# A hand-ordered first stretch with two weight tiles in conversion, 32-column query products, and u stored from the scalar queue

## The chip, the cores and the metric

The kernel runs on one core of a Trainium2 chip. The metric is the device time of one execution in microseconds (us): the median of the runs shown, lower is better. A difference of about 0.5% is what a measurement of this kernel can tell from no change.

## What is computed

Three blocks follow one another, in float32: attention through 32 landmarks, then two mixers with a two-layer perceptron (MLP) each. The weights `U`, `V`, `w_ch1`, `w_ch2` arrive as float64 and are converted on the chip.

```python
# attention: q, k, v are (8, 8, 576, 64); q_lm, k_lm are means over 18 rows (32 landmarks)
A  = softmax(q    @ k_lm^T / 8)          # 576 x 32
Bm = softmax(q_lm @ k_lm^T / 8)          # 32 x 32
C  = softmax(q_lm @ k^T    / 8)          # 32 x 576
Z  = Bm^T / (norm1(Bm) * norminf(Bm))
for _ in range(6): Z = 2 * Z - Z @ Bm @ Z
x  = A @ Z @ C @ v                       # heads side by side: (8, 576, 512)
# mixer 1: a rank-32 product over the sequence, then the MLP
u  = x + (x^T @ U @ V)^T
x  = u + relu(u @ w_ch1) @ w_ch2         # 512 -> 2048 -> 512
# mixer 2: real part of a 2-d FFT, layer norm, then a second MLP
u  = x + real(fft2(x));  un = layernorm(u)
out = u + relu(un @ w2_ch1) @ w2_ch2
```

## The kernel before, in words

**The work.** The attention runs batch by batch (class `Batch`, eight batches). The MLPs run over nine chunks of 512 columns (`NC`, `NCH`), the 8 x 576 rows of the sequence laid end to end. Each MLP takes two passes, since half of its weights fit at a time: passes 0 and 1 are the first MLP, passes 2 and 3 the second. A chunk has eight up blocks (`Mlp.up`, L205, 12 matmuls of 128x512 each, L212 to L214) and four down blocks (L248 to L272, 24 matmuls each, L257 to L259). Each matrix is held as a high part and a rest, so each product is three matmuls. `Mlp.stream` (L221) is a generator: one step for each up block and two for each down block, `STEPS` = 16 for a chunk.

**The conversion.** A weight tile of 128x512 is converted by `convert` (L87): a DMA into the raw tile `wraw`, four DVE operations (L97, L98, L101, L104), one ACT operation (L102), an addition on POOL (L106), a DVE operation (L108), then a cast on ACT and a subtraction on POOL in `split` (L51, L52). Its scratch tiles `cva` and `cvp` have one buffer each. In pass 0, `direct` (L880) converts 16 tiles straight into the MLP's weights. The tiles of the later passes are converted by `stage` (L113) and put in DRAM.

**The order.** Batch 0 and the first half of batch 1 run in 32 steps before the MLP starts (`FIRST`, L888, the loop at L896). There the Tile scheduler orders the instructions of each engine by its own costs. From L903 on, `tc.manual_schedule()` keeps the order of the program. In each step the loop runs one step of the MLP, the attention steps that `Slots` has for it (`Batch.steps`, L619: pairs of a step number and a method), and some conversion steps. Batch b starts 16 (b - 2) steps after the MLP does, so that batch b + 1 runs beside chunk b.

**The hand-over from a batch to a chunk.** `Batch.mix` (L601) makes four tiles `u1T` of 128x576; ACT (L609) and DVE (L610) each copy one half out of PSUM. Then SP issues the store to `u1`: three stores of 128 rows (L612, L614), one of 127 rows (L616) and one of one row (L617), because the rows of `u` have an order of their own. The chunk's tiles `xf` come back from `u1` by SP (L139, `ByBatch.get`), and `split_x` (L193) makes the high part on ACT (L51) and the rest on DVE or POOL (L52). Two of the four splits of the next chunk stand in the down block d = 2, and two in d = 3.

**The query products.** `query` (L486) multiplies blocks of 128 query columns by the landmarks (L498), and `mixed` (L543) multiplies the attention weights by `U` (L550), both with 128 columns of weights at a time. `values` (L467) makes its products with 32 columns of weights (L479), each into another 32 partitions of the result.

Of the kernel before, what the change touches and what calls it, by code (L numbers as in the profile page):

```python
# [23 lines left out]
P = 128  # L24
# [15 lines left out]
def body(ctx: ExitStack, tc: tile.TileContext, qT, kT, vn, mU, mV, w11, w12, w21, w22,  # L40
# [13 lines left out]
    def from_f64(pool, dst, w, n, pp=P):  # L54
# [3 lines left out]
        a = pool.tile([P, 512], U32, name="cva", bufs=1)[0:pp, 0:n]  # L58
        p = pool.tile([P, 512], U32, name="cvp", bufs=1)[0:pp, 0:n]
# [27 lines left out]
    def convert(cv, src, out, lag=0):  # L87

        raw = cv.tile([P, 512], U64, name="wraw", bufs=2)
        nc.sync.dma_start(raw, src)  # L90
        yield 1
        yield from wait(lag)
        u = raw.bitcast(U32).rearrange("p (n two) -> p n two", two=2)
        lo, hi = u[:, :, 0], u[:, :, 1]
        a = cv.tile([P, 512], U32, name="cva", bufs=1)
        p = cv.tile([P, 512], U32, name="cvp", bufs=1)
# [8 lines left out]
        yield 1  # L105
# [7 lines left out]
    def stage(cv, src, dst):  # L113
        st = cv.tile([P, 2, 512], F32R, name="stg", bufs=1)
        yield from convert(cv, src, st, 4)
        yield from wait(1)
        nc.sync.dma_start(dst, f32(st))
# [45 lines left out]
    class Mlp:  # L163
# [36 lines left out]
        def start(self):  # L200
            self.nx = []
            self.xf = self.load(0, self.passes[0][0])
            yield from self.split_x(self.xf)
# [85 lines left out]
    def attention_constants(cp, t):  # L289
        nc.sync.dma_start(ident_sb, ident)  # L290
        for nm, src, n in (("mask", mask, 64), ("bones", bones, P), ("istack", istack, R)):
            t[nm] = cp.tile([P, n], F32, name=nm + "_sb")
            nc.sync.dma_start(t[nm], src)
        t["U"] = cp.tile([P, 5, R], F32, name="U_sb")
# [3 lines left out]
        for nm in ("kb", "qb"):  # L298
            t[nm] = cp.tile([P, 4, 64], F32, name=nm)
            nc.gpsimd.memset(t[nm], 0.0)  # L300
# [5 lines left out]
    def attention_setup(t, pool, cvp):  # L306
        uraw = cvp.tile([P, 512], U64, name="wraw", bufs=2)[:, 0:5 * R].rearrange("p (t r) -> p t r", r=R)
# [5 lines left out]
        vst = pool.tile([P, S], F32, name="E", bufs=2)[0:R]  # L313
        for n in range(3):
            c = slice(n * S // 3, (n + 1) * S // 3)
            vraw = cvp.tile([P, 512], U64, name="wraw", bufs=2)[0:R, 0:S // 3]
# [8 lines left out]
    class Batch:  # L325
# [5 lines left out]
        EJ = [slice(0, 64), slice(64, P)]  # L331

# [127 lines left out]
        def scores_tail(self):  # L460
# [4 lines left out]
            nc.vector.tensor_copy(self.ETt, ps[0:64, 0:2 * P].rearrange("p (g c) -> p g c", g=2))  # L465
# [20 lines left out]
        def query(self, n):  # L486
# [528 lines left out]
```

## Time and profile before

| | |
|---|---|
| median of 3 runs | 2053.39 us (2045.59 to 2053.95) |
| the profiled execution | 2051.87 us |
| its span | 2050.1 us |
| busy, share of the span | PE 94%, DVE 46%, ACT 26%, POOL 17% |
| granted TensorE clock, mean | 0.979 of full speed |
| DMA | 262 MB, mean 128 GB/s |

The span is the time from the first to the last instruction that the profiler saw; about 1.8 us lie around it. PE, PEld, DVE, ACT, POOL and SP are the engines: matmul, weight load, vector, scalar, GpSimd and the queue that issues most DMAs. An L number is a line of the kernel. PE is busy nearly all the time from 220 us on. Before that, the page's slices of 51 us show it at four to eight tenths.

### The profile page before, as it was taken

What the parts mean: (1) busy time and instruction counts of PE and PEld (TensorE: products, weight loads), DVE (VectorE), ACT (ScalarE), POOL (GpSimd) and SP (SyncE); (2) the same over time, 40 slices, a digit from 0 to 9 for tenths busy, and PEclk for the clock granted to TensorE, in tenths of its full rate; (3) what the DMA queues carried; (4) which work ended last, traced back from release to release, by engine and by line L of the source; (5) the groups of instructions that cost most, each with busy time, mean ns of one, the idle gap of its engine ahead of it and who ended that gap; (6) DMA issues with size and microseconds to landing.
All of it is one profiled execution on the core that took longest, in us unless ns stands there. A gap on an engine that the chain in (4) does not pass through costs nothing.

```text
span 2050.1 us, 24963 instructions
## 1 busy us (share of the span) xinstructions
PE 1936.9 (94%) x9656; PEld 1578.3 (77%) x9656; DVE 949.0 (46%) x1682; ACT 532.8 (26%) x1089; POOL 358.4 (17%) x346
## 2 busy tenths in 40 slices
PE   4848999999999989999999999999999999999998
PEld 3636777877877878888788787888788888888887
DVE  5664744655553333454654654654432223333333
ACT  2332322322221222232332323433322221111110
POOL 2241110111111112222322222222111110000000
PEclk9869999999999999999999999999999999999999
DMA  5332352244212563343543663432422452432322
GB/s 179 118 129 76 101 163 93 101 137 145 91 57 94 175 233 126 131 150 101 178 149 106 236 226 99 157 125 79 151 82 83 170 185 93 125 122 88 93 93 77
DMA packets 145863, 262.17 MB, mean 128 GB/s; under 512 B 22768, under 2 KB 77904, under 8 KB 145744
## 3 DMA queue, kind: packets, MB, share of 16 engines
q1 hardware_dynamic: 145744, 260.58, 37.7%
q8 instruction: 76, 1.25, 0.3%
q14 instruction: 43, 0.35, 0.1%
HBM read 166.93 MB, written 93.59 MB: 127 GB/s over the span
## 4 chain that ended last, share of the span: by engine, by line
PE 74%; DVE 5%; DMA 5%; issue 4%; SPq 2%; POOL 1%; ACT 1%; DVEq 0%; POOLq 0%; ACTq 0%
PE ps L212 11%; PE ps L214 11%; PE ps L213 11%; PE ps L257 10%; PE ps L259 10%; PE ps L258 10%; DMA xf<-u 4%; SPq L617 1%; PE ps_f L77 1%; PE ps_f L76 1%; PE ps_f L78 1%; PE ps_n L607 1%; PE ps_n L566 1%; POOL x L52 1%; PE ps_c L440 1%
## 5 line engine op out<-in xcount | busy, mean ns | idle before, releaser
L212 PE MATMUL ps<-x,w 128*128 128x512 f32 x1152 | 465.9, 404 | 11.5 <-DVE g L217 6.6
L257 PE MATMUL ps<-g,w 128*128 128x512 f32 x1152 | 462.6, 402 | 2.0 <-DVE g L217 2.0
L214 PE MATMUL ps<-x,w 128*128 128x512 f32 x1152 | 454.5, 395 | 3.8 <-POOL x L52 1.8
L213 PE MATMUL ps<-x,w 128*128 128x512 f32 x1152 | 452.3, 393 | 0.0
L259 PE MATMUL ps<-g,w 128*128 128x512 f32 x1152 | 451.8, 392 | 0.0
L258 PE MATMUL ps<-g,w 128*128 128x512 f32 x1152 | 451.2, 392 | 0.0
L217 DVE SCALAR_TENSOR_TENSOR g<-ps,g 128x512 fp32r<-128x512 f32 x288 | 198.7, 690 | 461.6 <-ACT g L216 461.4
L216 ACT ACTIVATE g<-ps 128x512 fp32r<-128x512 f32 x288 | 171.8, 597 | 699.1 <-PE ps L214 698.7
L212 PEld LDWEIGHTS ps<-x,w 128*128 128x128 f32 x1152 | 218.8, 190 | 61.2 <-DVE g L217 7.0
L214 PEld LDWEIGHTS ps<-x,w 128*128 128x128 f32 x1152 | 218.0, 189 | 57.1 <-POOL x L52 6.6
L257 PEld LDWEIGHTS ps<-g,w 128*128 128x128 f32 x1152 | 217.7, 189 | 50.6 <-issue 4.4
L259 PEld LDWEIGHTS ps<-g,w 128*128 128x128 f32 x1152 | 217.6, 189 | 47.5
L213 PEld LDWEIGHTS ps<-x,w 128*128 128x128 f32 x1152 | 219.0, 190 | 43.2
L258 PEld LDWEIGHTS ps<-g,w 128*128 128x128 f32 x1152 | 218.1, 189 | 43.2
L52 POOL TENSOR_TENSOR x<-xf,x 128x512 fp32r<-128x512 f32 x72 | 97.0, 1352 | 633.7 <-ACT x L51 625.2
L266 DVE TENSOR_TENSOR xf<-ps,xf 128x512 f32<-128x512 f32 x108 | 74.4, 689 | 239.7 <-PE ps L259 236.9
L106 POOL TENSOR_TENSOR cvp<-cvp,cva 128x512 f32<-128x512 f32 x64 | 84.7, 1323 | 470.8 <-DVE cvp L104 456.9
L52 DVE TENSOR_TENSOR x<-xf,x 128x512 fp32r<-128x512 f32 x72 | 57.0, 791 | 157.5 <-ACT x L51 157.2
L51 ACT CAST x<-xf 128x512 fp32r<-128x512 f32 x144 | 85.1, 617 | 94.9 <-DMA xf<-u 94.0
L52 POOL TENSOR_TENSOR stg<-cva,stg 128x512 fp32r<-128x512 f32 x48 | 63.0, 1313 | 137.3 <-ACT stg L51 135.9
L102 ACT ACTIVATE wraw<-wraw 128x512 f32<-128x512 f32 x64 | 43.2, 675 | 94.6 <-DVE cva L98 84.7
L108 DVE SCALAR_TENSOR_TENSOR cva<-wraw,cvp 128x512 f32<-128x512 f32 x64 | 46.8, 732 | 22.6 <-POOL cvp L106 22.5
(271 smaller groups left out, 1797.7 us busy)
## 6 DMA issues: line engine op xcount, KB each, us to landing
wraw<-w SPq DMA_DIRECT2D x64, 512.0 KB
d<-stg SPq DMA_DIRECT2D x48, 512.0 KB
w<-d SPq DMA_DIRECT2D x48, 512.0 KB
y<-xf SPq DMA_DIRECT2D x72, 256.0 KB
xf<-y SPq DMA_DIRECT2D x72, 256.0 KB
U<-x SPq DMA_DIRECT2D x8, 1152.0 KB
u<-U SPq DMA_DIRECT2D x8, 1152.0 KB
un<-Z SPq DMA_DIRECT2D x16, 576.0 KB
```

Source lines behind the costliest of these rows:

```text
L51: nc.scalar.copy(hi, src)
L52: (eng or nc.vector).tensor_tensor(lo, src, f32(hi), op=ALU.subtract)
L106: nc.gpsimd.tensor_tensor(pf, pf, af, op=ALU.add)
L212: nc.tensor.matmul(ps, wh, xh, start=k == 0, stop=False)
L213: nc.tensor.matmul(ps, wl, xh, start=False, stop=False)
L214: nc.tensor.matmul(ps, wh, xl, start=False, stop=k == 3)
L216: nc.scalar.activation(g[:, 0, :], ps, AF.Relu)
L217: nc.vector.scalar_tensor_tensor(out=g[:, 1, :], in0=ps, scalar=0.0, in1=f32(g[:, 0, :]), op0=ALU.max, op1=ALU.subtract)
L257: nc.tensor.matmul(ps, wh, gh, start=k == 0, stop=False)
L258: nc.tensor.matmul(ps, wl, gh, start=False, stop=False)
L259: nc.tensor.matmul(ps, wh, gl, start=False, stop=k == HM - 1)
L266: nc.vector.tensor_tensor(res[d], ps, res[d], op=ALU.add)
```

## The change

- The 32 steps before the MLP stand in the hand-given order too (`tc.manual_schedule()` now begins before them).
- `convert` has two buffers of `cva` and `cvp` in pass 0 and three steps in place of five. The new `direct` keeps up to two tiles in conversion: the first half of tile i + 1 is issued ahead of the second half of tile i. Up to s = 0 two or three conversion steps are issued in each step, then three (five before).
- Raw tiles are fetched four tiles ahead. The first 14 lie in the buffers of the MLP's `g` tiles, which are free until the MLP starts.
- `query` and `mixed` use four products with 32 columns of weights in place of one with 128.
- Three copies out of PSUM go from DVE to ACT: `ETt`, the second half of `at`, and the second half of `u1T`.
- The five stores of `u1T` are issued by ACT (`nc.scalar.dma_start`) in place of SP.
- The pool `cv` of the later passes is opened after the pools of the attention are closed.

```diff
-    def convert(cv, src, out, lag=0):
-        raw = cv.tile([P, 512], U64, name="wraw", bufs=2)
-        nc.sync.dma_start(raw, src)
-        yield 1
-        yield from wait(lag)
-        u = raw.bitcast(U32).rearrange("p (n two) -> p n two", two=2)
+    def convert(cv, raw, out, bufs=1):
+        u = raw.rearrange("p (n two) -> p n two", two=2)
...
-        a = cv.tile([P, 512], U32, name="cva", bufs=1)
-        p = cv.tile([P, 512], U32, name="cvp", bufs=1)
+        a = cv.tile([P, 512], U32, name="cva", bufs=bufs)
+        p = cv.tile([P, 512], U32, name="cvp", bufs=bufs)
...
         nc.vector.scalar_tensor_tensor(out=pf, in0=lo, scalar=2.0 ** -52, in1=pf, op0=ALU.mult, op1=ALU.mult)
-        yield 1
         nc.gpsimd.tensor_tensor(pf, pf, af, op=ALU.add)
...
-            nc.vector.tensor_copy(self.ETt, ps[0:64, 0:2 * P].rearrange("p (g c) -> p g c", g=2))
+            nc.scalar.copy(self.ETt, ps[0:64, 0:2 * P].rearrange("p (g c) -> p g c", g=2))
...
-                        nc.tensor.matmul(ps[:, i * P + 64 * e:i * P + 64 * e + 64],
-                                         self.q[:, 2 * n + e, i * P:(i + 1) * P], kb[:, 2 * n + e, :], start=True,
-                                         stop=True)
+                        o = ps[:, i * P + 64 * e:i * P + 64 * e + 64]
+                        for r in self.QUARTERS:
+                            nc.tensor.matmul(o[r], self.q[:, 2 * n + e, i * P + r.start:i * P + r.stop],
+                                             kb[:, 2 * n + e, :], start=True, stop=True, skip_group_check=True)
...
-            nc.vector.tensor_copy(at[64:P, 2 * g + 1, 0:512], ps[64:P])
+            nc.scalar.copy(at[64:P, 2 * g + 1, 0:512], ps[64:P])
...
-            nc.vector.tensor_copy(u1T[:, HS:S], pss[1][:, 0:HS])
+            nc.scalar.copy(u1T[:, HS:S], pss[1][:, 0:HS])
             if i < 2:
-                nc.sync.dma_start(u[i * P:(i + 1) * P, :], u1T)
+                nc.scalar.dma_start(u[i * P:(i + 1) * P, :], u1T)
...
-                nc.sync.dma_start(u[385:512, :], u1T[0:127])
-                nc.sync.dma_start(u[256:257, :], u1T[127:128])
+                nc.scalar.dma_start(u[385:512, :], u1T[0:127])
+                nc.scalar.dma_start(u[256:257, :], u1T[127:128])
...
-        def direct(nm):
-            for i in range(HM):
-                yield from convert(cv, srcs[0][i + (HM if nm == "w2" else 0)], mlp.weight(nm))
+        def direct():
...
+            for _ in range(4):
+                fetch()
+            yield 1
+            live = []
+            for i in range(len(ws)):
+                fetch()
+                live.insert(0, convert(cv0, raws[i], ws[i], 2))
+                for _ in range(2):
+                    for g in list(live):
+                        if next(g, 0) == 0:
+                            live.remove(g)
+                        else:
+                            yield 1
...
-            for s in range(FIRST, 0):
-                if s == FIRST + Batch.LAST + 1:
-                    start = mlp.start()
-                slots.run(s)
-                if s > FIRST + Batch.LAST:
-                    next(start, 0)
-                some(convs, 3)
             with tc.manual_schedule():
...
+                for s in range(FIRST, 0):
+                    slots.run(s)
+                    if s == X0:
+                        mlp.start()
+                    elif X0 + 2 < s:
+                        some(mlp.more, 2)
+                    some(convs, 0 if s < FIRST + 4 else 3 if s < FIRST + 10 or s > X0 else 2)
...
                     if s < HM:
-                        some(convs, 5)
+                        some(convs, 3)
```

Two places show what the order becomes. The first is DVE's row just ahead of the second up block of chunk 0, before the change; `g` is the up block's result, and L217 its second part. Four whole conversions stand between the first and the second L217; this is the end of the third and the fourth:

```order
L108 SCALAR_TENSOR_TENSOR cva_952<-wraw_950,cvp_953 128x512
L97 TENSOR_SCALAR cva_990<-wraw_988 128x512
L98 SCALAR_TENSOR_TENSOR cva_990<-wraw_988,cva_990 128x512
L101 TENSOR_SCALAR cvp_991<-cva_990 128x512
L104 SCALAR_TENSOR_TENSOR cvp_991<-wraw_988,cvp_991 128x512
L108 SCALAR_TENSOR_TENSOR cva_990<-wraw_988,cvp_991 128x512
L217 SCALAR_TENSOR_TENSOR g_1052<-ps_1039,g_1052 128x512
```

The same place on DVE with the change (L218 is the former L217, L96 to L106 the conversion):

```order
L218 SCALAR_TENSOR_TENSOR g_1129<-ps_1116,g_1129 128x512
L576 TENSOR_TENSOR ry_1139<-ps_n_1140,ry_1099 128x2x64
L359 TENSOR_REDUCE ls_1145<-k__860 128x64
L96 TENSOR_SCALAR cva_1151<-g_903 128x512
L97 SCALAR_TENSOR_TENSOR cva_1151<-g_903,cva_1151 128x512
L106 SCALAR_TENSOR_TENSOR cva_1107<-g_863,cvp_1108 128x512
L218 SCALAR_TENSOR_TENSOR g_1169<-ps_1156,g_1169 128x512
```

Between the `g` of two up blocks there is now one half of one tile and one half of another.

The second place is the hand-over of batch 2 to chunk 2 on SP before the change; `u1_2` is the batch's result in DRAM, `xf` the tiles of the chunk:

```order
L616 DMA u1_2_64<-u1T_1971 127x576
L617 DMA u1_2_64<-u1T_1971 1x576
L349 DMA k__1986<-kT 128x1152 x2
L117 DMA d1_1_113<-stg_1664 128x1024
L90 DMA wraw_1991<-w11 128x512
L139 DMA xf_1993<-u1_1_63 128x128
L139 DMA xf_1993<-u1_2_64 128x384
L139 DMA xf_1994<-u1_1_63 128x128
```

With the change the same two stores stand in ACT's queue, behind the copies of `u1T` and ahead of the copies of `ET` and the casts of `x`; on SP the loads of `xf` follow right behind those of `k`:

```order
L615 COPY u1T_2190<-ps_n_2191 128x288
L616 COPY u1T_2190<-ps_n_2193 128x288
L622 DMA u1_2_64<-u1T_2190 127x576
L623 DMA u1_2_64<-u1T_2190 1x576
L461 COPY ET_2238<-ps_c_2233 128x512
L461 COPY ET_2259<-ps_c_2254 128x512
L468 COPY ETt_2264<-ps_b_2261 64x256
L51 CAST x_2279<-xf_2208 128x512
```

The store of 127 rows no longer stands ahead of the loads of `xf` in SP's queue; ACT passes it and the one-row store before it copies `ET`.

## Rows read from the trace of the kernel before

**Rows 1.** Busy time by stage, the whole core (stretches in us).
```profile
core 0: us, PE busy (x) PEld busy (x) DVE busy (x) ACT busy (x) POOL busy (x), PEclk, DMA share, GB/s
0.00:105.20 105.20, 66.31 (x414) 48.28 (x414) 66.16 (x162) 31.28 (x76) 29.87 (x45) 0.93 0.44 151
105.20:218.40 113.20, 79.65 (x444) 62.56 (x445) 64.00 (x132) 31.30 (x67) 31.11 (x30) 0.82 0.33 107
218.40:733.00 514.60, 494.51 (x2870) 401.89 (x2870) 255.16 (x527) 135.32 (x308) 74.81 (x89) 0.98 0.34 115
265.00:290.00 25.00, 20.46 (x180) 16.98 (x179) 8.30 (x18) 4.21 (x8) 1.27 (x1) 0.86 0.62 189
733.00:760.00 27.00, 20.42 (x84) 16.43 (x84) 7.33 (x12) 5.88 (x10) 0.72 (x1) 0.87 0.92 325
```
**Rows 2.** PE's waits, 0 to 760 us: us in total, times, longest.
```profile
PE ps_b L550 <- ACT at L541: 20.6, 1, 20.6
PE ps_b L505 <- DVE ry L483: 14.9, 5, 4.5
...
PE ps L212 <- DVE g L217: 6.6, 1, 6.6
```
**Rows 3.** Timeline of PE: first up block of chunks 0, 1 and 2.
```profile
105.22 0.80 PE L212 MATMUL ps<-x,w 128*128 128x512 f32 x1 [2.75 <-ACT x L51]
...
218.42 0.52 PE L212 MATMUL ps<-x,w 128*128 128x512 f32 x1
...
292.99 0.53 PE L212 MATMUL ps<-x,w 128*128 128x512 f32 x1
```
**Rows 4.** DVE's last conversion step, L108, before the first MLP matmul: us, busy (x).
```profile
0.00:105.20 105.20, 5.50 (x8) 0.93 0.44 151
```
**Rows 5.** Timeline of DVE, 122 to 146 us: one conversion and the next.
```profile
124.82 0.43 DVE L97 TENSOR_SCALAR cva<-wraw 128x512 uint32<-128x512 uint32 x1 [2.09 <-POOL w L52]
...
131.25 0.43 DVE L97 TENSOR_SCALAR cva<-wraw 128x512 uint32<-128x512 uint32 x1 [2.02 <-POOL w L52]
```
**Rows 6.** Timeline of POOL, 116 to 170 us: the same conversion.
```profile
127.24 1.26 POOL L106 TENSOR_TENSOR cvp<-cvp,cva 128x512 f32<-128x512 f32 x1 [2.46 <-DVE cvp L104]
129.96 1.26 POOL L52 TENSOR_TENSOR w<-cva,w 128x512 fp32r<-128x512 f32 x1 [1.45 <-ACT w L51]
```
**Rows 7.** The chain that ended last, 255 to 285 us: start, us, what.
```profile
261.72 0.24 SPq L616
...
262.01 4.86 SPq L617
...
269.86 11.88 DMA xf<-u
...
283.68 0.70 PE ps_b L505 x8
```
**Rows 8.** SP's waits, 262 to 284 us.
```profile
SPq L139 <- DMA u<-u1T: 4.4, 1, 4.4
```
**Rows 9.** Timeline of SP, 275 to 279 us: the loads of xf after that wait.
```profile
275.72 3.18 SPq L139 DMA_DIRECT2D xf<-u  x4
```
**Rows 10.** The one-row store L617 on SP: ns min/median/max of its issue.
```profile
L617 SPq DMA_DIRECT2D u<-u1T x8: 1094/4478/5522, 87.0 to 620.5; - x8
```
**Rows 11.** Timeline of ACT, 262 to 269 us.
```profile
264.85 0.59 ACT L458 COPY ET<-ps_c 128x512 f32<-128x512 f32 x1 [3.74 <-PE ps_c L456]
```
**Rows 12.** Timeline of PE, 244 to 296 us: products of 32 and of 128 columns.
```profile
270.93 0.65 PE L479 MATMUL ps_b<-v__1566,ET 128*32 128x64 f32 x32
...
272.58 2.00 PE L498 MATMUL ps_c<-kb,q__1597 128*128 128x64 f32 x16
```
**Rows 13.** Groups of PE by shape, 296 to 310 us: `mixed` of one batch.
```profile
L550 PE MATMUL ps_b<-U_sb,A 128*128 128x32 f32 x16 | 2.1, 272 | 0.0
```
**Rows 14.** The chain that ended last, 600 to 770 us.
```profile
738.30 12.15 DMA big<-tabs
```
**Rows 15.** Groups by shape, 0 to 760 us: ACT's copies of half u1T.
```profile
L609 ACT COPY u1T<-ps_n 128x288 f32<-128x288 f32 x32 | 12.7, 396 | 31.7 <-PE ps_n L607 31.7
```

More of the change, by code (lines that the diff above doesn't have):

```diff
@@ L111, in convert, with stage @@
         yield 1
-    def stage(cv, src, dst):
+    def stage(cv, src, dst, bufs):
+        raw = cv.tile([P, 1024], U32, name="wraw", bufs=2)
+        fetch_raw(raw, src)
+        yield from wait(5)
         st = cv.tile([P, 2, 512], F32R, name="stg", bufs=1)
-        yield from convert(cv, src, st, 4)
+        yield from convert(cv, raw, st, bufs)
         yield from wait(1)
@@ L202, in start @@
             self.xf = self.load(0, self.passes[0][0])
-            yield from self.split_x(self.xf)
+            self.more = self.split_x(self.xf)
         def up(self, m, x):
@@ L290, in attention_constants @@
         nc.sync.dma_start(ident_sb, ident)
+        t["U"] = cp.tile([P, 5, R], F32, name="U_sb")
+        for nm in ("kb", "qb"):
+            t[nm] = cp.tile([P, 4, 64], F32, name=nm)
+            nc.gpsimd.memset(t[nm], 0.0)
         for nm, src, n in (("mask", mask, 64), ("bones", bones, P), ("istack", istack, R)):
@@ L331, in body @@
         EJ = [slice(0, 64), slice(64, P)]
+        QUARTERS = [slice(32 * h, 32 * h + 32) for h in range(4)]
         def __init__(self, pool, psb, t, b):
@@ L549, in mixed @@
                 for i in range(4):
-                    nc.tensor.matmul(o, self.A[:, 512 * g + i * P:512 * g + (i + 1) * P], U[:, i, :], start=i == 0,
-                                     stop=False, skip_group_check=True)
+                    for r in self.QUARTERS:
+                        c = 512 * g + i * P
+                        nc.tensor.matmul(o[r], self.A[:, c + r.start:c + r.stop], U[:, i, :], start=i == 0,
+                                         stop=False, skip_group_check=True)
                 for sl in self.EJ:
@@ L871, in body, with staging, fetch @@
               (UN, None, ByChunk(y2), staged[2]), (UN, ByChunk(y2), Y, staged[3])]
-    def staging(cv, p):
-        return chained([stage(cv, srcs[p][i], staged[p][i]) for i in range(2 * HM)])
+    def staging(cv, p, bufs=1):
+        return chained([stage(cv, srcs[p][i], staged[p][i], bufs) for i in range(2 * HM)])
     N = NCH * STEPS
-    with pool("mm") as mp, pool("cv") as cv, pool("pm", space=PSUM) as pm:
+    with pool("mm") as mp, pool("pm", space=PSUM) as pm:
         mlp = Mlp(mp, pm, 3, passes)
-        def direct(nm):
-            for i in range(HM):
-                yield from convert(cv, srcs[0][i + (HM if nm == "w2" else 0)], mlp.weight(nm))
-        with pool("aa") as ap_, pool("ac") as ac, pool("pt", space=PSUM) as psb:
+        def direct():
+            ws = [mlp.weight(nm) for nm in ("w1", "w2") for _ in range(HM)]
+            raws = []
+            def fetch():
+                i = len(raws)
+                if i < len(ws):
+                    if i < EARLY:
+                        raw = f32(mp.tile([P, 2, 512], F32R, name="g", bufs=HM)).rearrange(
+                            "p a n -> p (a n)").bitcast(U32)
+                    else:
+                        raw = cv0.tile([P, 1024], U32, name="wraw", bufs=2)
+                    fetch_raw(raw, srcs[0][i])
+                    raws.append(raw)
+            for _ in range(4):
[9 more added lines that the diff above has]
+                            live.remove(g)
+                        else:
+                            yield 1
+            for g in live:
+                yield from g
+        EARLY = 14
+        with pool("aa") as ap_, pool("ac") as ac, pool("cv0") as cv0, pool("pt", space=PSUM) as psb:
             t = {}
@@ L908, in body @@
                     if s < HM:
[L909 removed]
+                        some(convs, 3)
+                        if s == HM - 1:
+                            some(convs, 99)
                     else:
                         some(later, 2 if s % 4 == 0 else 1)
[L912 to L914 removed]
+                some(later, 999)
+                some(gen, 9)
+        with tc.manual_schedule(), pool("cv") as cv:
             with pool("fp") as fp, pool("fc") as fc, pool("pf", space=PSUM) as psb:
```

36 lines of the change are left out of this document (17 added, 19 removed).

## The prediction, on record before the changed kernel was run

> **What bounds the kernel now.** I read the stages first (busy time and granted clock of each stretch), then PE's waits, then the chain that ended last at the places where PE waits, then the timelines there. From 218 to 733 us PE is busy in 494.51 of 514.60 us [rows 1]: the reader is to see that this stage, and what follows it, can gain little but for short holes. The first 218.4 us are another matter. Up to the first MLP matmul at 105.22 us [rows 3] PE is busy in 66.31 us, and in chunk 0, which lasts from there to 218.42 us, in 79.65 of 113.20 us at a granted clock of 0.82, a mix of the levels 2.4 and 1.2 GHz [rows 1]. Three kinds of holes explain most of what PE loses.
>
> The first is the conversion. PE's longest wait is one of 20.6 us for an ACT copy [rows 2]. In that time conversions go one at a time: L97 of one tile starts at 124.82 and of the next at 131.25 us, 6.43 us on, released by POOL's last step [rows 5], since each tile's scratch is free only then [rows 6]. Four of them stand in the queues ahead of the eviction that PE needs.
>
> The second is the hand-over from a batch to a chunk. The store of 127 rows is issued at 261.7 us, L617 holds SP for 4.86 us, and an `xf` load at 269.86 us takes 11.88 us to land; ACT's cast and DVE's subtraction wait for it, and with them PE until 283.68 us [rows 7]. SP itself waits 4.4 us for that store in the middle of its loads [rows 8] and goes on with them at 275.72 us [rows 9]. PE waited 14.9 us in five such places [rows 2], and after each the clock is lower: 0.86 from 265 to 290 us, against 0.98 over the stage [rows 1].
>
> The third is at the change of pass: DVE's queue stands behind `big<-tabs`, 12.15 us in the chain [rows 14], and PE waits 6.6 us [rows 2].
>
> **The change, part by part.** *To the first MLP matmul: no gain.* In both orders eight tiles are converted ahead of the splits of `x` (eight L108 before 105.2 us [rows 4]; in the new order eight casts of `w1` stand ahead of the first cast of `x`). So DVE, busy in 66.16 us there [rows 1], has the same conversions to do. Its copies of `u1T` leave it (four for batch 0, now on ACT at some 396 ns each [rows 15]), but newton steps of batch 1 and a split of `x` now stand ahead of the first up block, and ACT has L617's hold in its queue. I put the first matmul at 107 us; bounds 100 (the two-deep conversion shortens batch 0's chain) and 120 us (a strict order that waits wherever one engine is late).
>
> *Chunk 0.* An undisturbed chunk with attention is 292.99 - 218.42 = 74.6 us [rows 3] less its own hand-over, 25.00 - 20.46 = 4.5 us of hole and 0.14 x 25 = 3.5 us of clock [rows 1]: 66.5 us. Eight conversions are left for it. DVE needs 0.43 + 0.69 + 0.43 + 0.69 + 0.69 = 2.9 us for each (0.43 for L97 and L101, as L97 shows [rows 5], 0.69 for the other three, as L108 shows with 5.50 / 8 [rows 4]), 23 us in all, and POOL 1.26 + 1.26 us [rows 6]. With two tiles in flight a tile needs no longer wait for the other's last POOL step, so its cost is DVE's share: about half of the 23 us falls on top of a chunk whose DVE is half free (255.16 of 514.60 us [rows 1]). 66.5 + 11 = 77.5 us. Chunk 1 then starts at 184.5, say 185 us, for 218.4: **-33.4 us**. Ends: 100 + 66.5 gives -52; conversions that still go one by one, 0.
>
> *The hand-overs after chunk 0.* From 218.4 to 733 us PE's holes are 514.60 - 494.51 = 20.1 us and the clock costs 0.02 x 514.6 = 10.3 us [rows 1], 30.4 together, nearly all at hand-overs. With the store on ACT's queue the first loads of `xf` no longer stand behind 127 rows on SP's. The 14.0 us from its issue to the end of SP's wait (261.72 [rows 7] to 275.72 us [rows 9]) remain for the halves of `xf` that read those rows; they are cast in the next down block, one block of 24 matmuls later. I take three quarters: **-23 us**. Ends: -30.4 and 0.
>
> The store's cost moves to ACT: five issues, and L617's hold of 4.48 us in the median [rows 10]. Behind it stands the copy of `ET`, ready at 264.85 us after 3.74 us of idle ACT [rows 11]. If the hold ends near 267 us, the copy is 2 us late, and the products that read it start at 270.93 us [rows 12]. So it costs nothing while this cover lasts. The copies moved to ACT lie in the same idle time.
>
> *Change of pass.* The order of the changed kernel puts the first `tabs` load ahead of chunk 6's last stores, far from its cast. From 733 to 760 us PE loses 27.00 - 20.42 = 6.6 us and 0.13 x 27 = 3.5 us of clock [rows 1]; two further `tabs` loads still follow the weights, so I take 8 of the 10: **-8 us**. Ends: -10 and 0.
>
> *Products of 32 columns.* Sixteen L498 records take 2.00 us, and `query` has two such groups in a batch; 32 records of 32 columns take 0.65 us [rows 12]. 128 of those in place of 32: 4 x 0.65 = 2.6 us for 2 x 2.00. For `mixed`, 64 in place of 16: 1.3 for 2.1 us [rows 13]. That is 2.2 us for a batch; the six batches whose products fall beside MLP work on a busy PE give 13 us, of which I take 12, as other row groups may cost a little at each change: **-12 us**. Ends: -13 and 0.
>
> *No price:* fetching raw tiles early and the fewer steps in `convert` of later passes; both lie beside a busy PE, and if their cover went, a fetch late by a few us would hold one conversion.
>
> Sum, against the profiled execution's 2051.87 us: -33.4 - 23 - 8 - 12 = -76.4, so 2051.87 - 76.4 = 1975.5 us. The median of the runs shown, 2053.39, is 0.07% higher; I forecast **1976 us**. By the bounds of its terms it may lie from 1962 to 1990.
>
> **Rivals.**
>
> *The first stretch stays as long.* Strict order costs at the start what two-deep conversion gains. For it: DVE, ACT and POOL hand each tile to one another three times, and ACT now waits there for all of them. Against it: the same number of tiles in each part. Without the first term: 1976 + 33 = 2009 us.
>
> *The moved store saves only SP's time.* If the load and the store meet on the same DMA engines whoever issues them, and the 127 rows hold up `xf` there, the hand-overs stay. For it: the `xf` load of 269.86 us landed only at 281.7, 6 us after SP's wait for the store was over [rows 7, 9], so not the order of the queue alone sets it. Against it: that load was issued behind the store in one queue, with two more transfers between them. Without the second term: 1976 + 23 = 1999 us. The Trainium skill has this rule: DMA: Bandwidth & Descriptors, section "Issuing engines are not separate DMA queues", says that starting DMAs from several engines saves only the sequencer's issue time; by it the sum would be this rival's. The same page's "Queues, rings and completion order" says that each DMA engine takes turns between queues, which speaks for my forecast; no run so far shows either.
>
> *ACT is held until the store has landed.* If L617's hold is that of a full queue, ACT stands still for H us at each of eight batches, and `ET` is copied late; PE's products at 270.93 us, 9 us after the issue, wait about H - 7 us with the copies, and the clock adds some 2 us. The change is slower from 8 x (H - 5) = 76 us on, H = 14.5 us. The store's own 14.0 us would just not do; shared with SP's loads it could take up to twice that, and at the middle, 21 us, the cost is 8 x 16 = 128 us: 1976 + 128 = 2104 us. Against it: on SP the hold was 5.5 us at most [rows 10], far below the 14.0.
>
> *Everything goes.* All holes close and chunk 0 starts at 100 us: -52 - 30 - 10 - 13 = -105, 1947 us.
>
> *The small products gain nothing*, because the change of column groups eats it, so that this part doesn't do what it says: 1976 + 12 = 1988 us.
>
> **How the numbers follow.** Forecast 0.50, first stretch as long 0.16, store saves only SP's time 0.12, everything goes 0.12, small products gain nothing 0.06, ACT held 0.04. The range of 8 in 10 takes in all but the held ACT and the outer halves of the first stretch's rival and of the best case: 1947 to 2010 us. 0.5% is 10 us, about what a measurement of this kernel can tell: faster means below 2043. Faster 0.92; the same 0.04 (a held ACT with H near 14, or two rivals together); slower 0.04.
>
> **What would show it.** Right: the first L213 near 107 us and chunk 1's near 185; no PE wait over 3 us between them; L96 of consecutive tiles 3 to 5 us apart; at the hand-overs no PE wait for the `ry` of `values`, with the first cast of `x` within 4 us of its load; L623 on ACT below 6 us; `query` at 1.3 us a group; no PE wait over 2 us at the change of pass. Wrong: chunk 1 starting after 200 us, `xf` still landing 10 us after its issue, or ACT's `ET` copy more than 8 us after L622.

## The result, and the profile after

The changed kernel takes 2015.76 us (median of four runs, 2012.02 to 2018.09), where the kernel before takes 2049.81 (four runs, one more than in the table ahead, 2045.59 to 2053.95): a ratio of 0.9831, 95% interval 0.9808 to 0.9855. Forecast were 1976 us and a range from 1947 to 2010: the sign is right, the size is about half, and the range is missed. The profiled execution took 2012.02 us, 39.9 less than the one before. (One execution each of the runs e5 and e9 below, at a mean granted clock of 0.56, is left out of the comparisons.)

The stages of the changed kernel by the same view as [rows 1]: first the stretches of those rows, then its own, up to its first up block, chunk 0, chunks 1 to 6, chunks 7 and 8.

```profile
core 0: us, PE busy (x) PEld busy (x) DVE busy (x) ACT busy (x) POOL busy (x), PEclk, DMA share, GB/s
0.00:105.20 105.20, 53.57 (x654) 36.73 (x654) 70.33 (x160) 35.45 (x87) 32.43 (x48) 0.71 0.45 162
105.20:218.40 113.20, 92.53 (x727) 72.69 (x728) 68.95 (x134) 37.52 (x85) 30.20 (x33) 0.85 0.35 118
218.40:733.00 514.60, 500.89 (x3694) 402.51 (x3693) 245.63 (x498) 157.29 (x355) 80.03 (x92) 1.00 0.41 134
...
0.00:116.20 116.20, 54.74 (x658) 37.91 (x659) 78.44 (x176) 38.63 (x92) 36.91 (x51) 0.69 0.50 175
116.20:201.90 85.70, 74.86 (x587) 57.81 (x585) 52.71 (x105) 28.44 (x66) 24.80 (x25) 0.88 0.26 86
201.90:594.90 393.00, 382.03 (x3241) 305.28 (x3240) 205.72 (x440) 130.95 (x314) 54.52 (x74) 1.00 0.36 121
594.90:685.80 90.90, 88.16 (x386) 71.83 (x385) 28.90 (x44) 19.42 (x33) 15.77 (x14) 1.00 0.53 167
```

In the first 105.2 us PE does less than before (53.57 us for 66.31 [rows 1]), at a lower clock (0.71 for 0.93), and the first MLP matmul comes 11 us later; after that chunk 0 is shorter. The timeline of PE gives the starts of chunks 0, 1 and 2, the answer to [rows 3]:

```profile
116.22 0.88 PE L213 MATMUL ps<-x,w 128*128 128x512 f32 x1
...
201.87 0.88 PE L213 MATMUL ps<-x,w 128*128 128x512 f32 x1
...
271.60 0.53 PE L213 MATMUL ps<-x,w 128*128 128x512 f32 x1
```

The first matmul of every chunk, read from PE's timeline over the whole span, splits the difference of 39.9 us by stage (us):

| | before | change | difference | forecast |
|---|---|---|---|---|
| start of the first MLP matmul | 105.2 | 116.2 | +11.0 | +1.8 |
| chunk 0 | 113.2 | 85.65 | -27.55 | -35.7 |
| chunks 1 to 6 | 418.0 | 393.0 | -25.0 | -35 with chunks 7 and 8, hand-overs and products |
| chunks 7 and 8 | 93.45 | 90.9 | -2.5 | (in the line above) |
| first chunk of pass 1 | 51.8 | 43.5 | -8.3 | -8 |
| from there to the end | 1268.4 | 1280.9 | +12.5 | 0 |

What PE waits for up to chunk 1, and one line of DVE's waits there:

```profile
PE ps_n L572 <- DVE ry L576: 27.5, 7, 10.6
PE ps_b L482 <- ACT ETt L468: 13.1, 2, 9.0
PE ps_b L376 <- POOL qb L361: 10.5, 2, 9.5
```

```profile
DVE cva L96 <- POOL w L52: 18.6, 9, 5.1
```

The one wait of 20.6 us [rows 2] is gone; in its place PE waits seven times for the newton steps of batches 0 to 2 (`ry`), which stand in DVE's strict order behind conversions, and DVE itself stands 18.6 us in front of conversions whose buffer POOL has not freed. The longest, 10.6 us, ends 1.2 us ahead of the first MLP matmul; on DVE, the tile that waits for POOL and the `ry` behind it:

```profile
110.76 1.47 DVE L96 TENSOR_SCALAR cva<-g 128x512 uint32<-128x512 uint32 x1 [2.66 <-POOL w L52]
...
114.69 0.28 DVE L576 TENSOR_TENSOR ry<-ps_n,ry 128x128 f32<-128x128 f32 x1
```

The hand-over of batch 2, by the chain, by ACT's timeline and by SP's:

```profile
245.41 18.26 DMA u<-u1T
...
264.11 2.61 DMA xf<-u
```

```profile
245.69 8.77 ACTq L623 DMA_DIRECT2D u<-u1T  x1
254.50 1.07 ACT L461 COPY ET<-ps_c 128x512 f32<-128x512 f32 x2 [9.11 <-issue]
```

```profile
246.07 19.36 SPq L140 DMA_DIRECT2D xf<-u  x8
```

The store of 127 rows now takes 18.3 us (14.0 before by [rows 7, 9]), the one-row store behind it holds ACT for 8.8 us, and SP's eight loads of `xf` stretch over 19.4 us, since four of them stand behind SP's wait for it. While it runs alone, the 16 DMA engines are busy in 0.07 of their time, about as much as one engine in sixteen:

```profile
253.00:263.00 10.00, 8.86 (x237) 6.85 (x235) 5.21 (x11) 3.58 (x7) 0.55 (x1) 1.00 0.07 27
```

### The profile page after: what moved, and what is told of

Read it like the earlier page. It is cut to its first block, busy times and chain, and to the rows that moved or that the text cites. A ratio compares the mean times of both kernels' runs of the same rounds, so it can differ in the third digit from the quotient of the medians.

```text
span 2010.2 us, 27239 instructions
## 1 busy us (share of the span) xinstructions
PE 1902.5 (95%) x10808; PEld 1542.6 (77%) x10808; DVE 940.0 (47%) x1626; ACT 553.0 (28%) x1145; POOL 354.3 (18%) x346
## 4 chain that ended last, share of the span: by engine, by line
PE 75%; DVE 7%; DMA 7%; issue 3%; POOL 3%; ACT 2%; ACTq 0%; SPq 0%; POOLq 0%; DVEq 0%
PE ps L215 12%; PE ps L213 12%; PE ps L214 11%; PE ps L258 10%; PE ps L260 10%; PE ps L259 10%; DMA u<-u1T 5%; PE ps_f L76 1%; PE ps_f L77 1%; PE ps_f L78 1%; PE ps_n L613 1%; PE ps_n L572 1%; DMA wraw<-w 1%; POOL x L52 1%; DMA xf<-u 1%
## 5 line engine op out<-in xcount | busy, mean ns | idle before, releaser
L218 DVE SCALAR_TENSOR_TENSOR g<-ps,g 128x512 fp32r<-128x512 f32 x288 | 198.9, 691 | 455.2 <-ACT g L217 454.0
L217 ACT ACTIVATE g<-ps 128x512 fp32r<-128x512 f32 x288 | 171.9, 597 | 677.3 <-PE ps L215 676.9
L215 PEld LDWEIGHTS ps<-x,w 128*128 128x128 f32 x1152 | 218.3, 189 | 60.8 <-POOL x L52 12.8
L52 POOL TENSOR_TENSOR x<-xf,x 128x512 fp32r<-128x512 f32 x72 | 97.0, 1352 | 382.2 <-ACT x L51 380.5
L52 DVE TENSOR_TENSOR x<-xf,x 128x512 fp32r<-128x512 f32 x72 | 56.0, 778 | 115.5 <-ACT x L51 115.2
L52 POOL TENSOR_TENSOR stg<-cva,stg 128x512 fp32r<-128x512 f32 x48 | 66.6, 1388 | 124.6 <-ACT stg L51 123.3
L572 PE MATMUL ps_n<-ry 128*128 128x192 f32 (+1 forms) x192 | 44.3, 359 | 33.8 <-DVE ry L576 33.8
L101 ACT ACTIVATE wraw<-wraw 128x512 f32<-128x512 f32 x50 | 34.1, 682 | 144.8 <-DVE cva L97 137.7
```

The source lines that it names most:

```text
L52: (eng or nc.vector).tensor_tensor(lo, src, f32(hi), op=ALU.subtract)
L215: nc.tensor.matmul(ps, wh, xl, start=False, stop=k == 3)
L217: nc.scalar.activation(g[:, 0, :], ps, AF.Relu)
L218: nc.vector.scalar_tensor_tensor(out=g[:, 1, :], in0=ps, scalar=0.0, in1=f32(g[:, 0, :]), op0=ALU.max, op1=ALU.subtract)
```

## The experiments

Twelve more kernels ran; the kernel before took 2050.24, 2050.09 and 2051.91 us (medians) beside them. "Chunk 1" is the start of its first up block, "chunks 1 to 6" the time from there to that of chunk 7; both are from PE's timeline, and the loss of chunks 1 to 6 is told against 378.7 us, what they take where PE never waits (e1).

| run | median us | ratio to before, 95% interval | first matmul | chunk 1 | chunks 1 to 6 | start of pass 1 to end |
|---|---|---|---|---|---|---|
| before | 2050 | | 105.2 | 218.4 | 418.0 | 1320.2 |
| the change | 2015.8 | 0.9831 (0.9808 to 0.9855) | 116.2 | 201.9 | 393.0 | 1324.4 |
| e1 split store | 1988.3 | 0.9699 (0.9681 to 0.9717) | 115.2 | 194.1 | 378.7 | 1324.4 |
| e2 fifth step | 2005.9 | 0.9785 (0.9765 to 0.9804) | 116.5 | 197.5 | 400.3 | 1311.5 |
| e3 wide products | 2026.1 | 0.9884 (0.9865 to 0.9904) | 122.0 | 204.7 | 399.9 | 1323.9 |
| e4 store on SP | 2049.0 | 0.9990 (0.9976 to 1.0004) | 117.3 | 202.7 | 419.9 | 1323.9 |
| e5 split, fifth step | 1973.5 | 0.9632 (0.9607 to 0.9656) | 114.9 | 193.4 | 378.7 | 1310.8 |
| e6 split, one tile | 2000.2 | 0.9762 (0.9738 to 0.9786) | 120.7 | 205.3 | 378.7 | 1326.7 |
| e7 split, scheduler | 1963.2 | 0.9581 (0.9557 to 0.9606) | 80.6 | 170.1 | 378.7 | 1324.1 |
| e8 split, seven tiles | 1990.6 | 0.9715 (0.9690 to 0.9740) | 96.3 | 197.9 | 378.7 | 1323.6 |
| e9 split, fifth, scheduler | 1951.7 | 0.9510 (0.9491 to 0.9529) | 81.2 | 170.4 | 378.7 | 1311.1 |
| e10 before, split store | 2016.0 | 0.9822 (0.9807 to 0.9837) | 103.3 | 212.6 | 393.5 | 1322.2 |
| e11 scheduler alone | 1994.2 | 0.9718 (0.9698 to 0.9737) | 84.3 | 181.5 | 393.1 | 1327.7 |
| e12 split, scheduler, one tile | 1987.2 | 0.9684 (0.9656 to 0.9711) | 78.0 | 191.9 | 378.7 | 1323.7 |

**e1, the store of 127 rows in two.** Base: the change.

```diff
-                nc.scalar.dma_start(u[385:512, :], u1T[0:127])
+                nc.scalar.dma_start(u[385:497, :], u1T[0:112])
+                nc.scalar.dma_start(u[497:512, :], u1T[112:127])
```

> The changed kernel, with the store of 127 rows of u1T cut into one of 112 rows and one of 15; all else as in the change. In the changed kernel's trace that store takes 18 us, SP waits 17.7 us for it before it loads the other xf tiles, and ACT is held 6.8 to 8.8 us by the one-row store behind it. Theory A (the store runs on one DMA engine, and this alone keeps the hand-overs): both pieces land within 5 us, SP waits under 5 us, ACT is held under 3 us, the first MLP matmul moves from 116 to about 109 us, and chunks 1 to 6 lose 8 to 12 us of holes and clock: 1995 to 2003 us for 2016. Rival B (the other transfers beside it slow it): it still lands after more than 12 us, 2010 to 2020 us. Rival C (the store becomes quick, but the chain of cast, subtraction and softmax behind the loads sets the holes): SP's wait goes and the time stays at 2010 to 2018 us.

It gained 27.5 us in the medians, more than theory A asked. The last store's issue (its line is one lower here) no longer holds ACT, by the view of that line, and PE has no hole in chunks 1 to 6, by the view of the stretch:

```profile
L624 ACTq DMA_DIRECT2D u<-u1T x8: 221/264/285, 88.3 to 557.9; - x8
```

```profile
194.10:572.70 378.60, 378.60 (x3240) 304.11 (x3239) 203.29 (x442) 133.72 (x317) 57.15 (x77) 1.00 0.38 129
```

264 ns in the median, for 7794 in the change. Theory A holds for the hand-overs: 14.3 us of chunks 1 to 6, 3.9 of chunk 7, 6.7 of chunk 0. It failed on the first matmul, which stays at 115.2: ACT's hold of 6.8 us there was not what puts it so late. In e1's chain from 88 to 114 us POOL's last step on one tile (L52) and DVE's first on the next (L96) follow each other four times, down to the `ry` that PE needs.

**e2, the fifth conversion step in the staged tiles.** Base: the change.

```diff
+        yield from wait(late)
         nc.gpsimd.tensor_tensor(pf, pf, af, op=ALU.add)
...
-        yield from convert(cv, raw, st, bufs)
+        yield from convert(cv, raw, st, bufs, 1)
```

> The changed kernel, with the conversion of the later passes given back its fifth step (a step between DVE's L103 and POOL's L104), so that a tile takes 11 steps as before and not 10; the first 16 tiles as in the change. Theory A (with 20 conversion steps for a chunk, 10 for a tile put the work of each second tile into the same steps at the end of a chunk, ahead of the splits of x on ACT and POOL, and that is what passes 1 and 2 lose): from the first matmul of pass 1 to the end 1311 to 1314 us, as in the kernel before without its wait at the change of pass, against 1324 in the changed kernel; 2002 to 2007 us for 2016. Rival B (the loss there is one run's clock, or comes from where the FFT's steps meet the earlier chunks): 1320 to 1327 us there, 2012 to 2019 us.

Theory A: 1311.5 us from pass 1 on, for 1324.4. (The text on the change ahead says that a conversion has three steps for five; as the code shows it has four.) The chunk of pass 1 that loses most begins at 876.4 us in the change. Its stretches, then ACT's timeline there:

```profile
876.40:886.40 10.00, 5.97 (x19) 3.49 (x17) 5.93 (x8) 3.46 (x8) 6.14 (x6) 0.76 0.42 139
886.40:896.40 10.00, 10.00 (x38) 7.79 (x38) 2.44 (x5) 1.54 (x5) 0.00 (x0) 0.73 0.76 244
896.40:943.60 47.20, 46.10 (x232) 38.33 (x231) 25.25 (x43) 12.62 (x24) 8.64 (x8) 1.00 0.19 65
```

```profile
874.20 0.68 ACT L101 ACTIVATE wraw<-wraw 128x512 f32<-128x512 f32 x1 [6.34 <-DVE cva L97]
874.77 0.60 ACT L51 CAST x<-xf 128x512 fp32r<-128x512 f32 x1
...
881.15 0.61 ACT L51 CAST stg<-cva 128x512 fp32r<-128x512 f32 x1
881.67 0.61 ACT L51 CAST x<-xf 128x512 fp32r<-128x512 f32 x1
```

and PE's matmul that needs the last of these casts:

```profile
882.33 0.79 PE L213 MATMUL ps<-x,w 128*128 128x512 f32 x1 [2.09 <-ACT x L51]
```

ACT stands 6.34 us at the conversion's L101, because DVE has long operations of the Fourier mixer ahead of L97 (L818, L819 and L692, 868.7 to 873.1 us), and the casts of `x` for the next chunk queue behind. PE then has holes, and the granted clock falls to 0.76 and 0.73, a mix of the levels 2.4 and 1.2 GHz, for twenty us. The same chunk of e2:

```profile
879.40:889.40 10.00, 8.90 (x43) 6.45 (x42) 4.93 (x9) 3.94 (x10) 2.79 (x3) 1.00 0.90 294
889.40:899.40 10.00, 10.00 (x50) 8.16 (x49) 4.61 (x9) 2.63 (x6) 1.29 (x1) 1.00 0.22 77
```

It lasts 60.8 us there, and 67.2 in the change. That ten steps for a tile and twenty for a chunk repeat the same meeting in each chunk is how I read it; the run shows only that the missing step costs it. In pass 0 the fifth step cost 7.3 us in chunks 1 to 6, and 3.9 us in all up to pass 1, so e5 has it in the later passes alone.

**e3, products of 128 columns again.** Base: the change.

```diff
-        QUARTERS = [slice(32 * h, 32 * h + 32) for h in range(4)]
+        QUARTERS = [slice(0, P)]
```

> The changed kernel, with the query products and the products of U in one piece of 128 columns again. Theory A (the prediction's term): 2.2 us more for a batch, chunks 1 to 6 longer by 12 to 14 us: 2027 to 2031 us for 2016. Rival B (32-column products gain nothing beside other work): 2013 to 2019 us. Rival C (more: the longer products lie in the chain that sets the first stretch): over 2032 us.

10.3 us slower in the medians, 11.9 up to pass 1: a microsecond under theory A's time, but chunks 1 to 6 grew by 6.9 us and not by 12 to 14. Their view shows why:

```profile
204.70:604.60 399.90, 395.94 (x2473) 323.90 (x2472) 204.01 (x440) 131.48 (x314) 53.96 (x75) 0.99 0.35 118
```

PE is busy for 13.9 us more than in the change, but the holes are 4.0 us and not 11.0. The shorter products gave PE time, and half of it went into waiting for the late store. With the store split on either side, where PE hardly waits, these chunks take 393.5 us with the products of 128 columns (e10) and 378.7 with those of 32 (e1), 14.8 less.

**e4, the stores back on SP.** Base: the change.

```diff
-                nc.scalar.dma_start(u[i * P:(i + 1) * P, :], u1T)
+                nc.sync.dma_start(u[i * P:(i + 1) * P, :], u1T)
...
-                nc.scalar.dma_start(u[385:512, :], u1T[0:127])
-                nc.scalar.dma_start(u[256:257, :], u1T[127:128])
+                nc.sync.dma_start(u[385:512, :], u1T[0:127])
+                nc.sync.dma_start(u[256:257, :], u1T[127:128])
```

> The changed kernel, with the five stores of u1T issued by SP again. The prediction: the hand-overs come back, +23 us, 2039 us. Theory A (the queue matters little at the hand-overs, since the store's own time sets them, and on ACT its hold delays the conversions of the first stretch): chunks 1 to 6 longer by 5 to 12 us, the first MLP matmul earlier by about 7 us (116 to 109), 2010 to 2022 us. Rival B (ACT's hold costs more than SP's, in the hand-overs too): 2003 to 2010 us.

33 us slower, and all of the change's gain is gone; both of my later theories fell, and the prediction was nearer. The view of chunks 1 to 6 and SP's hold at the one-row store:

```profile
202.70:622.60 419.90, 393.36 (x3240) 313.32 (x3240) 204.97 (x434) 129.81 (x312) 49.90 (x72) 0.96 0.33 111
```

```profile
L623 SPq DMA_DIRECT2D u<-u1T x8: 926/4721/5426, 87.5 to 606.6; - x8
```

Holes of 26.5 us and a clock of 0.96. So the queue does matter while the store is slow: on SP the loads of `xf` that don't need its rows stand behind it too. At the hand-over of batch 2, by SP's timeline and the chain, the store is issued, a load that doesn't need its rows lands 10.94 us after its issue, and SP goes on with the last four loads:

```profile
244.52 0.24 SPq L622 DMA_DIRECT2D u<-u1T  x1
...
258.37 3.22 SPq L140 DMA_DIRECT2D xf<-u  x4
```

```profile
250.97 10.94 DMA xf<-u
```

So on SP the store itself took 13.8 us.

**e10, the kernel before with nothing but the split store.**

```diff
-                nc.sync.dma_start(u[385:512, :], u1T[0:127])
+                nc.sync.dma_start(u[385:497, :], u1T[0:112])
+                nc.sync.dma_start(u[497:512, :], u1T[112:127])
```

> The kernel before the change, with the store of 127 rows cut into 112 and 15, still issued by SP: nothing else. In the kernel before, chunks 1 to 7 last 26 + 6 us longer than the work that PE has in them. Theory A (the one DMA engine under that store is the cause of these holes): chunks 1 to 6 last 392 to 397 us for 418, chunk 7 about 44 us; 2017 to 2026 us for 2050. Rival B (SP's order and the loads behind it set the hand-over as well): 2030 to 2045 us. Rival C (nothing, the store only hurts with the change's order): 2046 to 2054 us.

```profile
212.60:606.00 393.40, 393.17 (x2472) 321.29 (x2471) 221.28 (x477) 115.31 (x274) 57.26 (x74) 1.00 0.35 118
```

The stretch is that of its chunks 1 to 6: PE is busy in 393.17 of 393.40 us at full clock. Two lines make the kernel before some 36 us faster (2016.0 for 2051.9 on the same chip), as much as the whole change, and SP keeps the store. Theory A, the time a microsecond below its range: the one transfer was the cause of the hand-over's cost. Chunks 1 to 7 get 30.9 us shorter, as much as the 30.4 us that the prediction read as the loss there.

**e5, both repairs.** Base: the change, with the split of e1 and the step of e2 in `staging(cv, 2)` and `staging(cv, 3)` only.

```diff
+                nc.scalar.dma_start(u[385:497, :], u1T[0:112])
+                nc.scalar.dma_start(u[497:512, :], u1T[112:127])
...
+        yield from convert(cv, raw, st, bufs, late)
...
-                later, gen = staging(cv0, 1, 2), mlp.stream(0)
+                later, gen = staging(cv0, 1, 2, 0), mlp.stream(0)
```

> The changed kernel with the split store of the first of these runs, and with the fifth conversion step for the tiles of passes 1 to 3's stretch alone (the tiles converted in pass 0 keep four). Theory A (the two losses are apart: one in pass 0, one in passes 1 and 2): chunks of pass 0 as in the run with the split store (first matmul 115, chunk 1 at 194, pass 1 at 660 us), from there 1311 to 1313 us to the end: 1973 to 1979 us. Rival B (the later loss moves elsewhere when the earlier one goes): 1982 to 1990 us.

Theory A; the two losses are apart.

**e6, e8, e7, e11, e12: the first stretch.** All but e11 have the split store of e1, so e1 is what they are compared with. e6 takes the second tile out of conversion (`cva` and `cvp` also have one buffer in the conversion of `U` and `V` and in that of pass 1's tiles).

```diff
-                live.insert(0, convert(cv0, raws[i], ws[i], 2))
...
+                yield from convert(cv0, raws[i], ws[i], 1)
```

> The changed kernel with the split store, and with one tile in conversion at a time (one buffer of cva and cvp) in pass 0; the pace stays: as many tiles stand ahead of each up block. Compared with the run with the split store (first matmul 115.2, chunk 1 at 194.1 us). Theory A (two tiles at a time is what shortens the first stretch): chunk 1 starts 10 to 25 us later, at 204 to 219 us. Rival B (the order is what counts, spreading the conversions over the steps): chunk 1 at 191 to 199 us. Rival C (two at a time delays the attention's chain on DVE): the first matmul before 112 us.

Chunk 1 at 205.3, 11.2 us later than in e1: theory A, at its low end. e8 changes the pace.

```diff
-                    some(convs, 0 if s < FIRST + 4 else 3 if s < FIRST + 10 or s > X0 else 2)
+                    some(convs, 0 if s < FIRST + 4 else 3 if s < FIRST + 10 else 1 if s <= X0 else 3)
...
-                        some(convs, 3)
+                        some(convs, 5)
```

> The changed kernel with the split store, and with another pace: seven tiles and not eleven have their last DVE step ahead of the first g, the others follow in chunk 0 (one conversion step in each step of the middle stretch in place of two, five in each of the first eight steps of the MLP in place of three). Theory A (DVE's conversions ahead of it hold the first matmul, 2.9 us of DVE for each): four tiles, 11 to 12 us: first matmul at 103 to 106 us, chunk 0 longer by half of it, chunk 1 at 186 to 191 us for 194. Rival B (the attention's own chain through PE, ACT and DVE holds it): first matmul at 112 to 116 us and chunk 1 at 197 to 207 us. Rival C (both: earlier by 11 us, and all of it given back): chunk 1 at 192 to 196 us.

The first matmul came 19 us earlier, at 96.3, and chunk 0 took 22.6 us more: nearest to C, but with 3.8 us lost. Conversions ahead of the first matmul do hold it, but in the strict order moving them only moves the wait. e7 gives the 32 steps back to the scheduler: they move out of `tc.manual_schedule()`.

```diff
+            for what in "kq":
+                batches[0].load(what)
...
             with tc.manual_schedule():
-                for what in "kq":
-                    batches[0].load(what)
...
                 later, gen = staging(cv0, 1, 2), mlp.stream(0)
```

> The changed kernel with the split store, and with the scheduler's order in the 32 steps before the MLP, as before the change; two tiles in conversion as in the change. Theory A (the strict order waits where one engine is late, and this puts the first matmul at 115 and not 105): first matmul at 104 to 109 us, chunk 1 at 183 to 190. Rival B (eleven tiles in place of eight ahead of the first up block put it there, whoever orders them): 113 to 118 us, chunk 1 at 190 to 197. Rival C (the scheduler's order is worse): chunk 1 after 198 us.

Better than theory A: chunk 1 at 170.1 for 194.1, and 1963.2 us. DVE's longest group of waits in e1, and the same wait in e7, each up to chunk 1:

```profile
DVE cva L96 <- POOL w L52: 17.1, 10, 2.7
```

```profile
DVE cva L96 <- POOL w L52: 6.7, 4, 2.7
```

and PE's waits for `ry`, in e1 and in e7:

```profile
PE ps_n L572 <- DVE ry L576: 29.2, 6, 13.9
```

```profile
PE ps_n L572 <- DVE ry L576: 14.1, 6, 6.7
```

The stretches of e7 up to its first up block, and chunk 0:

```profile
0.00:80.60 80.60, 50.21 (x642) 33.73 (x642) 69.61 (x154) 34.73 (x85) 33.23 (x46) 0.75 0.71 242
80.60:170.10 89.50, 73.44 (x607) 56.31 (x601) 61.81 (x126) 33.00 (x74) 31.48 (x30) 0.94 0.30 96
```

DVE does the same 131 us of work up to chunk 1 (69.61 + 61.81 here, 78.44 + 52.71 in the change); the strict order lets it stand idle for longer. It also puts more ahead of the first MLP matmul: ten tiles have their last DVE step there in the change and in e1, eight in e7 and e11. e11 has the scheduler's order without the split store.

```diff
+            for what in "kq":
+                batches[0].load(what)
...
             with tc.manual_schedule():
-                for what in "kq":
-                    batches[0].load(what)
...
                 later, gen = staging(cv0, 1, 2), mlp.stream(0)
```

> The changed kernel with the scheduler's order in the 32 steps before the MLP and nothing else changed (127 rows in one store). Theory A (the strict order's price stands by itself, some 24 us up to the start of chunk 1): chunk 1 at 175 to 182 us for 202, 1988 to 1996 us for 2016. Rival B (ACT's hold behind the one-row store and the late xf then set the first stretch): chunk 1 at 186 to 198 us, 1998 to 2012 us.

Theory A: 20.4 us up to chunk 1, and 21.5 in the medians, is the strict order's price within the change. e12 is e7 with the edit of e6.

```diff
-                live.insert(0, convert(cv0, raws[i], ws[i], 2))
...
+                yield from convert(cv0, raws[i], ws[i], 1)
```

> The scheduled run with the split store, with one tile in conversion at a time (one buffer of cva and cvp) in pass 0. Theory A (two at a time is worth in the scheduler's order what it is worth in the strict one, 11 us): chunk 1 at 178 to 190 us for 170. Rival B (the scheduler fills the gaps with other work): chunk 1 at 166 to 174 us.

Chunk 1 at 191.9: two tiles at a time are worth 21.8 us in the scheduler's order, twice the 11.2 of the strict one, which is more than either theory said. What PE waits for there is the `at` of [rows 2] again, which in e7 costs it 0.6 us:

```profile
PE ps_b L556 <- ACT at L545: 27.8, 1, 27.8
```

e12 has neither two tiles nor the strict order, and still chunk 1 starts 20.7 us earlier than in the kernel before with the split store (e10, 212.6). That is the early fetch, the new pace, the work moved to ACT and the shorter products together; no run takes them apart.

**e9, the three edits that gained.** The edits of e5 and e7 together.

```diff
+                nc.scalar.dma_start(u[385:497, :], u1T[0:112])
+                nc.scalar.dma_start(u[497:512, :], u1T[112:127])
...
+        yield from convert(cv, raw, st, bufs, late)
...
+            for what in "kq":
+                batches[0].load(what)
...
             with tc.manual_schedule():
-                for what in "kq":
-                    batches[0].load(what)
```

> The changed kernel with the three edits that gained: the split store, the fifth conversion step in passes 1 and 2, the scheduler's order in the 32 steps before the MLP. Theory A (three places that don't touch): 1963 us of the scheduled run less the 13 to 15 us between the runs with the split store alone and with the fifth step: 1948 to 1952 us; first matmul near 81, chunk 1 near 170, pass 1 near 636 us. Rival B (they overlap): 1956 to 1965 us.

1951.7 us: the fastest here, 4.9% below the kernel before (interval 4.7 to 5.1), of which the change as it was brought 1.7.

## Why the prediction was wrong in size

**The first stretch, -33.4 forecast, -13.8 measured.** (That is the way from the kernel before to e3, 218.4 to 204.7 us; the shorter products bring 2.8 more.) This is the step that failed. In the scheduler's order the two-tile conversion does end the long wait of [rows 2] (e12 against e7), but it is worth 11.2 us in this order and 21.8 in the scheduler's, where I gave it the whole term. What I priced too low was the strict order itself: I gave the first matmul 107 us and kept 120 only as a bound, and put the rest of its price into a rival with a chance of 0.16. e11 prices it at 20.4 us, and without it chunk 1 starts at 181.5, beside the forecast's 185 (with it 201.9, past the 200 us set as a sign of being wrong); that is luck in part, for the first matmul then comes at 84.3 and not 107, and chunk 0 takes 97.2 us and not 77.5. One reading was wrong as well: I counted eight conversions ahead of the first matmul from ACT's casts, while DVE had ten done there (78.44 us of work for 66.16). And tiles don't start 3 to 5 us apart in chunk 0, as I said they would: DVE's timeline has them 7.6 and 7.8 us apart, since with two buffers L96 still waits for POOL's last step on an earlier tile.

```profile
128.13 0.43 DVE L96 TENSOR_SCALAR cva<-g 128x512 uint32<-128x512 uint32 x1 [2.06 <-POOL w L52]
...
135.72 0.43 DVE L96 TENSOR_SCALAR cva<-g 128x512 uint32<-128x512 uint32 x1 [2.71 <-POOL w L52]
...
143.47 0.43 DVE L96 TENSOR_SCALAR cva<-wraw 128x512 uint32<-128x512 uint32 x1 [0.48 <-POOL w L52]
```

**The hand-overs, -23 forecast.** From the kernel before to e3 chunks 1 to 8 shrink by 18.5 us; taking the move back (e4) costs 33. The term's direction and size were near; its cause was half seen. (The 33 us are not all a gain on the kernel before: there chunks 1 to 6 lost 24.5 us at the hand-overs, 418.0 less e10's 393.5, and with the rest of the change but the stores on SP they lose 41.2, 419.9 less 378.7.) I saw that the 14 us of the store remain and took three quarters of the holes all the same. The store got longer, 18.3 us, and the loss left over is 14.3 us in chunks 1 to 6 (393.0 less 378.7) and 3.9 in chunk 7. Of the 14.3, 11.0 are holes: 6.3 for `ry`, which by the chain waits for the late `xf`, and 4.3 for `ETt`, which waits for ACT. The rival that the moved store saves only SP's time is refuted as it stood, since the move saved 26.9 us in chunks 1 to 6 (e4 against the change), but its mechanism, a slow transfer that stays slow whoever starts it, is what remained. (That rival also counted two transfers between the store and the load of 269.86 us; the order of the kernel before has four, and a first load of `xf`.) The Trainium skill's rule that I weighed (DMA: Bandwidth & Descriptors, "Issuing engines are not separate DMA queues") fits the transfer and not the time: the store was no quicker from ACT, yet what stood behind it on SP was worth 33 us. The cause is that the 127 rows keep about one DMA engine of 16 busy: they take 18.3 us, at a share of 0.07 once they move alone, and as 112 and 15 rows they bring no such hold and no hole in chunks 1 to 6 (e1, e10). The Trainium skill states the rule (DMA: Bandwidth & Descriptors, "Why a DMA increments its semaphore by 16 and not by 1"): a DMA runs on the largest number of engines up to 16 that divides the slowest dimension of both its sides, here the rows, so 127 of them, a prime, run on one. The trace agrees.

**ACT held.** Forecast below 6 us, and a rival from 14.5 us on: measured 7.8 in the median, 8.8 at most, and the copy of `ET` starts 9.1 us after L622 at batch 2, one of the signs of being wrong. Its visible price is PE's wait for `ETt`, 9.0 us once up to chunk 1 and 4.3 us in four places after, a wait that e4 doesn't have in chunks 1 to 6. It is no more than a bound: without the hold (e1) the first matmul came only 1.1 us earlier.

**Products of 32 columns, -12: right in the number, by luck in part.** e3 says 11.9 up to pass 1. The forecast had all of it beside MLP work; chunks 1 to 6 gave 6.9, the first stretch 2.8 and chunks 7 and 8 2.2.

**Change of pass, -8: right.** 8.3 us. PE waits nowhere from 680 to 745 us, and the first `tabs` load is issued 89 us ahead of pass 1:

```profile
596.94 0.38 SPq L660 DMA_DIRECT2D big<-tabs  x1
```

Before, it came 8.4 us after pass 1's start [rows 14]. No run takes this edit alone.

**"No price: the fewer steps in `convert` of later passes": wrong by 12.5 us.** I named the cover, a busy PE, and did not follow the queue: a conversion operation that waits on ACT has the casts of `x` behind it. The fifth step brings all of it back (e2, e5).

The sum then reads -13.8 - 18.5 - 11.9 - 8.3 + 12.5 = -40.0, for the 39.9 measured. The two large misses, the first stretch and the fewer steps, have the same sign. The rival in which the first stretch gains nothing stood at 2009 us, inside the range; with the 12.5 us that had no price beside it, the time left the range. The narrower span of 1962 to 1990 us, "by the bounds of its terms", doesn't follow either: added up, those ends give 1947 to 2052.

## What to carry to other kernels

Before moving a slow transfer to another queue, ask why it is slow: the two lines that made 127 rows into 112 and 15 were worth as much as the whole change. A strict order needs a price of its own in the sum: count for each engine the work that stands ahead of the moment you forecast, on the engine that does it, and don't expect moved work to fill gaps by itself. And where a generator loses a step, every later place that it feeds has a new order, so look at what now stands in front of the operations that the busiest engine waits for.

## What was not expected of the hardware

The store of 127 rows took 18.3 us in the changed kernel and 14.0 before. The queue that it is issued from makes the difference: e4 is the changed kernel with the stores on SP, and there it took 13.8 us at the same hand-over. Why ACT's queue is slower is not shown. Once it ran alone, the core's DMA moved mostly 23 to 28 GB/s, where up to 252 us it had mostly 200 to 415:

```profile
GB/s 0 332 312 55 295 276 212 240 300 415 409 356 358 310 98 26 23 26 23 28 24 26 26 23 26 60 23 28 28 23 28 23 28 28 23 28 51 0 0 112
```

(the row of bandwidth from 245 to 265 us of the changed kernel, in slices of 0.5 us). The issue of one row behind it held its queue for 4.5 us in the median on SP [rows 10] and for 7.8 on ACT; behind 15 rows it took 0.26.
